# Attention and an ELU feed-forward layer in one kernel: more FFN1 row blocks as seven block products, sums and masks of two head pairs in one instruction, a new order of steps

## The chip, the cores and the metric

The kernel runs on one core of one Trainium2 chip. A core has five engines with queues of their own: TensorE (matmuls, PE in the profile; its weight loads are the row PEld), VectorE (DVE), ScalarE (ACT), GpSimd (POOL, which here starts most DMAs) and SyncE (SP, which starts the other DMAs). The metric is the device time of one execution in microseconds, lower is better. The kernel before took 335.11 us as the median of three runs.

## The reference

For 8 batches and 8 heads, causal attention over 576 positions with 16 beacon keys in front that every query sees, then a feed-forward layer over all 4608 tokens:

```python
B, H, S, Nb, D = (8, 8, 576, 16, 64)
...
scores = scale * np.matmul(q, k_all.transpose(0, 1, 3, 2))
...
scores = np.where(causal, -1000000000.0, scores)
...
a = np.exp(scores)
a /= a.sum(-1, keepdims=True) + 1e-09
return np.matmul(a, v_all).astype(np.float32)
...
x = np.ascontiguousarray(attn_out.transpose(0, 2, 1, 3)).reshape(B * S, H * D)
h = x @ w_in
g = np.where(h > 0.0, h, alpha * (np.exp(np.minimum(h, 0.0)) - 1.0))
return (g @ w_out).astype(np.float32)
```

w_in is 512 x 2048 and w_out 2048 x 512. The 16 + 576 = 592 keys make five blocks of 128 (the last of 80).

## The kernel before, in words

**One long list of steps.** The body defines small functions, each a step, and one string lists all steps in order; `run` calls them one after the other. Each engine takes its instructions from its own queue in that order and waits on semaphores only for data and for buffers. So the string sets which work stands ahead of which on every engine, DMA queues included. `F.4.10` is step F with the arguments 4 and 10.

**Attention.** Heads go in four pairs p, and two head pairs make a half g of a batch. `S` (L308) makes scores, keys on the partitions, in pieces of 2 x 512 columns; `x` (L335) is the exp on ScalarE into the tile `et`; `m` (L340, L346) multiplies the blocks on the diagonal by a triangle of ones on VectorE. A row of et has 1664 columns for one head pair, since keys of later blocks need only later queries: 576, 464, 336, 208 and 80 queries. `L` (L401) sums the exps over the keys: matmuls with a matrix of ones, four heads at a time in strips of 32 output rows (`quad`, L377), then some first products with V. For batches 3 to 7 (`b >= BD`) `D` (L386, L393) first adds the five key blocks on VectorE, so that one matmul per head (L419) does for queries from 112 on. For batches 0 to 2 the quads run over all blocks. `n` (L434, L437) makes 1/sum on ScalarE by Ln and Exp, `W` (L377) multiplies by V, and `M` (L471) scales and writes the tokens, transposed, into the tile xT.

q and k of batches 0 to 2 come by `lq` into staging tiles (qst, kst; two sets) and are transposed by TensorE (`T`). Those of batches 3 to 7 are copied as bf16 to DRAM (`lk`, POOL) and come back through DMA transposes (`lt`, SP, L777) into the second staging set; `lp` (L785, L786) adds the beacon keys there on POOL. `lv` (L141, L144, L149) loads V.

**Feed-forward.** Tokens go in tiles t of 512 (the first is split in two of 256, so t runs from 0 to 9). FFN1 in its plain form is `F` (L502, L511): one block of 128 of the 2048 hidden values, four matmuls of 512 columns into one PSUM bank `hps` (there are two). `e` (L521) and `u` (L526) read it on ScalarE as exp and relu, and `k` (L536) joins them on VectorE to ELU. Four consecutive blocks of hidden values make a row block g. For tiles 8 and 9 the row blocks 0 to 2 are done in another way: the product of the 2 x 2 blocks of weights and of tokens is made of seven block products instead of eight. `H` (L674) makes sums of the weight blocks once, `X` (L687, L690) sums of the token blocks for each tile, `P` (L698, L707) is one product, four matmuls of 256 columns, and a row block has seven (numbers 0 to 6). They alternate between the two banks of `hps`: 0, 2, 4 and 6 into one and 1, 3 and 5 into the other. Between products `K` takes a snapshot of the bank: a copy on ScalarE (L717) after 0, 2 and 3, an add of bank and snapshot on VectorE (L720) after 1, 4 and 5. `E`, `U` (L729, L736) and `V` (L746) are then exp, relu and ELU.

FFN2 is `G` (L557) for tiles 0 and 1. For tiles 2 to 9 it is made of seven block products as well: `Z` and `wt` (L578) make sums on VectorE, `Q` (L632) are the matmuls of 256 columns, and `J` (L646, L650, L653) takes the results out, and the output goes by SP (L656).

Of the kernel before, what the change touches and what calls it, by code (L numbers as in the profile page):

```python
# [9 lines left out]
FP16 = mybir.dt.float16  # L10
BF16 = mybir.dt.bfloat16
# [6 lines left out]
def kernel(  # L18
# [134 lines left out]

# [3 lines left out]
    def load_wi(c):  # L157
        f_ = slice(DF // 2 * c, DF // 2 * (c + 1))
        for g in range(2):
            for i in range(4):  # L160
                nc.gpsimd.dma_start(
                    out=w_in16[32 * i:32 * (i + 1), 2 * g:2 * g + 2, f_], in_=wi_v[i, :, g, :, f_])
# [18 lines left out]
    qks = [konst.tile([P, 2, P * NKC], BF16, name=f"qk{i}") for i in range(2)]  # L181
# [67 lines left out]
    @step  # L249
    def wi(c):  # L250
        load_wi(c)
# [133 lines left out]
    @step  # L385
    def D_(b, p, n, eng="v"):  # L386

        r_ = presum[b, p] = qks[p % 2].bitcast(FP16)[:, :, 0:S]
        t = et(b, p)
        a, e, col = next((a, e, col) for (j, a, e, col) in lays[b] if j == n + 1)  # L390
        rows = kc[n + 1]
        o = r_[0:rows, :, a:e]
        (nc.vector if eng == "v" else nc.gpsimd).tensor_tensor(  # L393
            out=o, in0=t[0:rows, :, a:e] if n == 0 else o, in1=t[0:rows, :, col:col + e - a], op=ALU.add)
# [6 lines left out]
    def L(b, g):  # L401
# [12 lines left out]
        else:  # L414
            t = hd[b, g] = psum.tile([P, 1024], FP32, tag="S", name="lt")
            r_ = lt[b, g] = t[:, 512 - QA:512 - QA + S]
            if b >= BD:
                for i in range(4):
                    nc.tensor.matmul(  # L419
                        out=r_[32 * i:32 * (i + 1), QA:S], lhsT=ones,  # L420
                        rhs=presum[b, 2 * g + i // 2][:, i % 2, QA:S], start=True, stop=True, skip_group_check=True)
# [246 lines left out]

    def rot(n_, t, g, i):
# [4 lines left out]
    def H_(n, g):  # L674
        c = slice(2 * g, 2 * g + 2)
        a11, a12, a21, a22 = (w5[:, j, :, c, i, :] for i in range(2) for j in range(2))
        o_, x_, y_, f_ = {1: (S1[:, :, c], a21, a22, ALU.add), 2: (S2[:, :, c], S1[:, :, c], a11, ALU.subtract),
                          4: (S4[:, :, c], a12, S2[:, :, c], ALU.subtract), 3: (a21, a11, a21, ALU.subtract)}[n]
# [19 lines left out]
    def P_(t, g, ph):  # L698
# [107 lines left out]
    L.0.A T.1.0.0 lv.0.0.1 n.0.A cq.1.0.0 m.0.0.3 T.1.1.0 W.0.A.0 W.0.A.1 M.0.A.0 M.0.A.1 m.0.1.3  # L806
    S.0.2.1 cb.1.2 ck.1.1.0 m.0.2.2 cb.1.0 S.1.5 m.0.2.3 x.0.2.1 wi.0 x.1.5 S.1.3 x.1.3 S.0.3.1
    x.0.3.1 S.0.3.2 x.0.3.2 F.0.1 e.0.1 S.1.1 r.0.1 g.0.1 S.1.4 x.1.4 F.0.0 S.1.2 F.0.2 x.1.1 x.1.2
    u.0.0 lv.0.3.4 lq.1.0.4.8 e.0.2 m.0.3.2 m.0.1.2 m.0.3.3 L.0.B n.0.B e.0.0 wi.1 W.0.B.0 M.0.B.0
    W.0.B.1 M.0.B.1 wo.0 r.0.2 T.1.2.0 F.1.1 ck.1.2.0 g.0.2 T.1.3.0 e.1.1 u.1.1 S.1.6 x.1.6 F.0.4  # L810
    F.1.7 e.0.4 k.0.0 cq.1.3.0 S.1.11 S.1.7 m.1.1.0 cb.1.3 r.0.4 g.0.4 e.1.7 r.1.7 lq.2.0.0.8
    G.0.0.0 x.1.7 F.0.5 x.1.11 e.0.5 S.1.12 g.1.7 cb.2.1 m.1.2.0 x.1.12 S.1.0 F.0.7 r.0.5 G.0.1.0
    S.1.8 x.1.0 g.0.5 F.1.5 e.0.7 x.1.8 m.1.3.1 S.1.10 cb.2.0 m.1.1.1 S.1.9 e.1.5 x.1.10 r.0.7 g.0.7
    cb.2.2 lv.1.0.1 wo.1 r.1.5 g.1.5 x.1.9 F.1.0 u.1.0 e.1.0 m.1.0.0 T.2.0.0 cq.2.0.0 F.0.3 T.2.1.0
    cq.2.1.0 T.2.2.0 e.0.3 u.0.3 m.1.2.1 k.0.3 wt.1.0 k.1.1 ck.2.2.0 F.1.4 F.0.6 e.0.6 S.2.0 S.2.5
    x.2.5 x.2.0 r.0.6 m.1.3.0 G.0.0.1 m.1.0.1 g.0.6 G.0.1.1 k.1.0 lv.1.2.3.4 lp.3.0 lp.3.1 T.2.3.0
    e.1.4 ck.2.3.0 L.1.1 n.1.1 F.1.2 r.1.4 u.1.2 e.1.2 M.1.1.0 W.1.1 M.1.1.1 S.2.3 F.1.3 x.2.3 L.1.0
    W.1.0 n.1.0 wo.2 M.1.0.0 M.1.0.1 u.1.3 e.1.3 wo.3 g.1.4 G.0.0.2 S.2.1 x.2.1 F.2.13 wt.1.1 e.2.13
    S.2.4 lk.3.0 lk.3.1 lt.3.0 x.2.4 S.2.8 x.2.8 k.1.2 cb.2.3 G.0.1.2 F.2.0 u.2.0 u.2.13 S.2.7 x.2.7
    k.1.3 S.2.9 x.2.9 e.2.0 G.0.0.3 o.0.0 G.0.1.3 F.2.3 e.2.3 S.2.10 m.2.0.0 S.2.2 r.2.3 g.2.3 k.2.0  # L820
    x.2.10 x.2.2 G.1.0.0 F.2.11 e.2.11 u.2.11 S.2.6 S.2.12 lv.2.2.3.4 x.2.6 F.2.1 u.2.1 e.2.1
    m.2.1.0 F.1.6 G.1.0.1 m.2.2.1 x.2.12 k.2.13 F.2.7 e.2.7 m.2.0.1 m.2.1.1 k.2.11 u.2.7 k.2.7 u.1.6
    lv.2.0.1 e.1.6 G.1.0.2 S.3.0 x.3.0 S.2.11 x.2.11 F.2.9 F.2.15 e.2.9 H.1.1 o.0.1 u.2.15 k.2.1
    k.1.6 m.2.3.0 e.2.15 L.2.0 W.2.0 n.2.0 F.2.12 m.2.3.1 r.2.9 g.2.9 M.2.0.1 lk.5.1 F.2.6 M.2.0.0
    G.1.0.3 lk.4.0 wt.2.0 wt.2.1 m.2.2.0 e.2.6 u.2.6 wt.4.1 s.0.0 s.0.1 u.2.12 e.2.12 k.2.15 S.3.2
    S.3.3 x.3.3 F.2.4 F.2.14 x.3.2 k.2.12 u.2.14 L.2.1 n.2.1 W.2.1 e.2.4 M.2.1.0 M.2.1.1 e.2.14
    u.2.4 G.1.1.0 S.3.4 F.2.2 lv.3.0.1 F.2.8 k.2.4 k.2.14 x.3.4 k.2.6 e.2.2 u.2.2 e.2.8 r.2.8
    m.3.0.1 S.3.1 o.1.0 k.2.2 lt.3.1 S.3.5 x.3.5 F.2.10 e.2.10 G.1.1.1 x.3.1 u.2.10 G.1.1.2 m.3.0.0
# [115 lines left out]
```

## Time and profile before

| | |
|---|---|
| runs, us | 336.85, 334.85, 335.11 (median 335.11) |
| the profiled execution | 337.32 us, its span 335.6 us |
| TensorE busy | 324.1 us, 97% of the span, 3559 matmuls |
| VectorE busy | 279.1 us, 83% |
| ScalarE busy | 282.4 us, 84% |
| GpSimd busy | 88.7 us, 26% |
| granted TensorE clock | 0.99 |

The profile is of one execution, and its span is what the engines show of it; the time includes a start and an end around it. A busy time counts overlapped instructions once. Matmuls are pipelined, so what one costs in a stream is the distance between starts in the timeline and not its own length. Idle time of an engine that nobody waits for costs nothing. A group's row has line, engine and operation, what it writes and reads with the shapes, the count, then busy us and the mean ns of one, then the idle time in front of it and who ended that.

### The profile page before, as it was taken

To read this page: it belongs to the slowest core of one execution; us is meant where nothing else is said; L and a number is where in the kernel's file an instruction comes from. 1 tells how busy PE (TensorE), PEld (TensorE's weight loads), DVE (VectorE), ACT (ScalarE), POOL (GpSimd) and SP (SyncE) were. 2 spreads that over 40 slices of the span, in tenths; PEclk is the share of its full clock that TensorE was granted. 3 is DMA by queue.
4 is the path that set the end of the run, shared out by engine and by line. 5 is a ranking of instruction groups with operands and counts; after the bars stand their busy time and mean duration, and the time that the engine had idled before them with its cause. 6 is when DMAs were issued, how large, how long until landed. Compare 5 with 4: busy or idle time off the path is not lost. (4 is left out here: it accounts for less than half of the span.)

```text
span 335.6 us, 8729 instructions
## 1 busy us (share of the span) xinstructions
PE 324.1 (97%) x3559; PEld 207.3 (62%) x3561; DVE 279.1 (83%) x592; ACT 282.4 (84%) x463; POOL 88.7 (26%) x121
## 2 busy tenths in 40 slices
PE   7978999999999999999999999999999999999995
PEld 3544766545445555656555666556656788788784
DVE  2662788658799899987999898997999999997971
ACT  2996798899999999989898989897997769879651
POOL 8857768360038404700080060000000000000000
PEclk9996999999999999999999999999999999999999
DMA  8999999999919995997199488000211021020123
GB/s 108 153 170 175 179 186 187 157 145 174 145 32 130 167 170 55 168 172 104 52 111 164 104 58 161 25 31 2 95 33 34 0 97 33 7 89 31 34 87 102
DMA packets 129080, 34.65 MB, mean 103 GB/s; under 512 B 112912, under 2 KB 127504, under 8 KB 129040
## 3 DMA queue, kind: packets, MB, share of 16 engines
q0 software_dynamic: 94912, 18.49, 68.3%
q1 hardware_dynamic: 33552, 15.47, 22.2%
q8 instruction: 28, 0.46, 0.6%
q10 hardware_dynamic: 576, 0.13, 0.2%
q14 instruction: 12, 0.10, 0.1%
HBM read 37.22 MB, written 15.34 MB: 157 GB/s over the span
## 5 line engine op out<-in xcount | busy, mean ns | idle before, releaser
L511 PE MATMUL hps<-xT,w_in 128*128 128x512 f16 (+1 forms) x544 | 120.1, 359 | 1.8 <-DMA w_in<-in_moe_w_in_dram 1.5
L335 ACT ACTIVATE et<-sc 128x1024 f16<-128x1024 f32 (+2 forms) x114 | 104.8, 977 | 5.8 <-PE sc L320 5.8
L632 PEld LDWEIGHTS <-gt 128*128 128x128 f16 x768 | 74.2, 98 | 18.6 <-issue 2.0
L521 ACT ACTIVATE e<-hps 128x512 f32<-128x512 f32 x120 | 72.4, 623 | 9.5 <-PE hps L511 7.9
L511 PEld LDWEIGHTS <-w_in 128*128 128x128 f16 x544 | 50.2, 99 | 46.4 <-issue 8.5
L536 DVE SCALAR_TENSOR_TENSOR gt<-e,r 128x512 f16<-128x512 f32 x108 | 71.7, 684 | 5.5 <-ACT r L526 3.5
L526 ACT ACTIVATE r<-hps 128x512 f16<-128x512 f32 x108 | 64.9, 624 | 7.3 <-PE hps L511 3.8
L632 PE MATMUL ops<-w_out,gt 128*128 128x256 f16 x368 | 47.9, 273 | 0.4 <-DVE osb L650 0.4
L632 PE MATMUL ops<-wt,gt 128*128 128x256 f16 x352 | 46.7, 273 | 0.1
L149 POOL DMA_DIRECT2D v<-in_v_dram x40 | 35.8, 1025 | 5.8 <-DMA w_out<-in_moe_w_out_dram 2.7
L340 DVE TENSOR_TENSOR et<-et,triu 128x512 f16<-128x512 f16 (+4 forms) x108 | 31.8, 332 | 1.7 <-ACT et L335 1.7
L578 DVE TENSOR_TENSOR gt<-gt 128x1024 f16<-128x1024 f16 x48 | 32.5, 685 | 0.5
L377 PEld LDWEIGHTS <-v 128*32 128x32 f16 (+1 forms) x800 | 17.0, 96 | 8.9 <-issue 1.1
L393 DVE TENSOR_TENSOR qk<-qk,et 128x672 f16<-128x672 f16 (+2 forms) x60 | 21.6, 368 | 0.8
L377 PE MATMUL ut<-et,v 128*32 128x464 f16 (+3 forms) x560 | 21.0, 296 | 0.0
L471 DVE TENSOR_TENSOR xT<-ut,rl 128x672 f16<-128x672 f32 (+12 forms) x26 | 16.4, 670 | 1.7 <-ACT rl L437 1.1
L653 DVE TENSOR_TENSOR osb<-ops,sm 128x512 f32<-128x512 f32 x23 | 15.7, 684 | 1.5 <-PE ops L632 1.3
L144 POOL DMA_DIRECT2D v<-in_beacon_v_dram x8 | 6.4, 795 | 37.7 <-PE ut L377 37.7
L557 PE MATMUL ops<-w_out,gt 128*128 128x512 f16 x64 | 16.0, 380 | 0.0
L746 DVE SCALAR_TENSOR_TENSOR gt<-e,r 128x512 f16<-128x512 f32 x24 | 16.0, 686 | 0.0
L632 PE MATMUL ops<-w_out,s 128*128 128x256 f16 x112 | 15.2, 273 | 0.0
L717 ACT COPY kst<-hps 128x512 f32<-128x512 f32 x18 | 10.3, 588 | 5.5 <-PE hps L707 5.3
(112 smaller groups left out, 406.1 us busy)
## 6 DMA issues: line engine op xcount, KB each, us to landing
out_dram<-osb SPq DMA_DIRECT2D x35, 256.0 KB, 2.3
v<-in_v_dram POOLq DMA_DIRECT2D x24, 128.0 KB, 8.2
scr<-in_q_dram POOLq DMA_DIRECT2D x5, 576.0 KB, 14.5
scr<-in_k_dram POOLq DMA_DIRECT2D x5, 576.0 KB, 16.1
w_in<-in_moe_w_in_dram POOLq DMA_DIRECT2D x16, 128.0 KB, 6.7
w_out<-in_moe_w_out_dram POOLq DMA_DIRECT2D x4, 512.0 KB, 9.5
v<-in_v_dram POOLq DMA_DIRECT2D x8, 112.0 KB, 9.7
v<-in_v_dram POOLq DMA_DIRECT2D x8, 80.0 KB, 8.2
```

The costliest lines, as they stand in the source:

```text
L149: nc.gpsimd.dma_start(out=vt[b][r0:r0 + n, j, :, :], in_=v[b, :, ilo[j]:ilo[j] + n, :].rearrange("h s d -> s h d"),)
L335: nc.scalar.activation(out=ets[b, d][:, :, a - EC2 * d:e - EC2 * d], in_=sc[b, g][:, :, a - c0:e - c0], func=AFT.Exp, bias=0.0, scale=SCALE)
L340: nc.vector.tensor_tensor(out=o, in0=o, in1=i, op=ALU.mult)
L377: nc.tensor.matmul(out=t[32 * i:32 * (i + 1), a - qa:e - qa], lhsT=ones[0:kc[j], :] if half is None else v16[0:kc[j], j, h, 32 * half:32 * ...
L393: (nc.vector if eng == "v" else nc.gpsimd).tensor_tensor(out=o, in0=t[0:rows, :, a:e] if n == 0 else o, in1=t[0:rows, :, col:col + e - a], ...
L471: nc.vector.tensor_tensor(out=x_tile(k)[:, 2 * g:2 * g + 2, tok - TT * k:to - TT * k], in0=u[:, :, o - qa:o - qa + w], in1=rls[b, g][:, o: ...
L511: nc.tensor.matmul(out=h[:, n_, :], lhsT=w_in16[:, cc, P * fc:P * (fc + 1)], rhs=xt[k][:, cc, a - TT * k:e - TT * k], start=(cc == 0), sto ...
L521: nc.scalar.activation(out=eb[t, i], in_=flat(hp[t, i]), func=AFT.Exp, bias=0.0, scale=1.0)
L526: nc.scalar.activation(out=rb[t, i], in_=flat(hp[t, i]), func=AFT.Relu, bias=0.0, scale=1.0)
L536: nc.vector.scalar_tensor_tensor(out=half(t, i), in0=eb[t, i], scalar=1.0, in1=rb[t, i], op0=ALU.subtract, op1=ALU.min)
L578: (nc.vector if eng == "v" else nc.gpsimd).tensor_tensor(out=o_, in0=a_, in1=b_, op=op_)
L632: nc.tensor.matmul(out=xy[t, n_][qd], lhsT=lw[:, P * qd:P * (qd + 1)], rhs=wt_[:, c, :], start=(first and c == 0 and (qd == 0 or (t, n_) n ...
```

## The change

1. Row block 0 of tiles 4 to 7 and row block 3 of tiles 8 and 9 go from F, e, u, k to P, K, E, U, V. X runs for tiles 4 to 7 too, and H for row block 3, whose weight sums lie in the q staging tile of the second set (`more`).
2. `D` takes two head pairs in one instruction, and runs for batches 1 and 2 too; L uses the result wherever there is one. The sums of batches 1 and 2 lie in the staging tiles, the others in `qk01`, which joins two tiles.
3. `m` takes two head pairs in one instruction, for batches from 1 on.
4. The beacon row of V is loaded behind the first block of V instead of ahead of all; `load_wi` and `load_v` are split, so that each DMA is a step of its own.
5. The string of steps has a new order. Up to `cq.1.3.0` it is the old one but for the split loads; from there on it is new.

```diff
     def load_v(b, js):
...
-            nc.gpsimd.dma_start(
-                out=vt[b][0:NB, 0, :, :], in_=beacon_v[b].rearrange("h n d -> n h d"))
         for j in js:
...
+            if j == 0:
+                nc.gpsimd.dma_start(
+                    out=vt[b][0:NB, 0, :, :], in_=beacon_v[b].rearrange("h n d -> n h d"))
...
-    qks = [konst.tile([P, 2, P * NKC], BF16, name=f"qk{i}") for i in range(2)]
+    qk01 = konst.tile([P, 2, 2, P * NKC], BF16, name="qk01")
+    qks = [qk01[:, i, :, :] for i in range(2)]
...
     def m(b, p, g):
 
-        t = et(b, p)
+        t = et(b, p) if b == 0 else None
         if b > 0:
-            m_ = lambda c: triu[:, c:c + 2, :].unsqueeze(1).broadcast_to([P, 2, 2, P])
+            t = ets[b, p].rearrange("p h (y c) -> p h y c", y=2)
+            m_ = lambda c: triu[:, c:c + 2, :].unsqueeze(1).unsqueeze(1).broadcast_to([P, 2, 2, 2, P])
...
-    def D_(b, p, n, eng="v"):
-
-        r_ = presum[b, p] = qks[p % 2].bitcast(FP16)[:, :, 0:S]
-        t = et(b, p)
+    def D_(b, g, n):
+
+        if b < BD:
+            r_ = stq[b % 2][g].bitcast(FP16)[:, 0:4 * S].rearrange("p (y i s) -> p y i s", y=2, i=2)
+        else:
+            r_ = qk01.bitcast(FP16)[:, :, :, 0:S]
+        presum[b, g] = r_
+        t = ets[b, g].rearrange("p i (y c) -> p y i c", y=2)
         a, e, col = next((a, e, col) for (j, a, e, col) in lays[b] if j == n + 1)
         rows = kc[n + 1]
-        o = r_[0:rows, :, a:e]
-        (nc.vector if eng == "v" else nc.gpsimd).tensor_tensor(
-            out=o, in0=t[0:rows, :, a:e] if n == 0 else o, in1=t[0:rows, :, col:col + e - a], op=ALU.add)
+        o = r_[0:rows, :, :, a:e]
+        nc.vector.tensor_tensor(
+            out=o, in0=t[0:rows, :, :, a:e] if n == 0 else o, in1=t[0:rows, :, :, col:col + e - a], op=ALU.add)
...
-            if b >= BD:
+            if (b, g) in presum:
                 for i in range(4):
                     nc.tensor.matmul(
                         out=r_[32 * i:32 * (i + 1), QA:S], lhsT=ones,
-                        rhs=presum[b, 2 * g + i // 2][:, i % 2, QA:S], start=True, stop=True, skip_group_check=True)
+                        rhs=presum[b, g][:, i // 2, i % 2, QA:S], start=True, stop=True, skip_group_check=True)
...
+    more = {id(y): stq[1][0].bitcast(FP16)[:, 512 * i:512 * (i + 1)].rearrange("p (k c f) -> p k c f", k=2, f=P)
+            for i, y in enumerate((S1, S2, S4))}
+
+    def wsum(y, g):
+        return y[:, :, 2 * g:2 * g + 2] if g < SG else more[id(y)]
...
-                lw = w5[:, a_[1], k_, 2 * g + c, a_[0], :] if isinstance(a_, tuple) else a_[:, k_, 2 * g + c, :]
+                lw = w5[:, a_[1], k_, 2 * g + c, a_[0], :] if isinstance(a_, tuple) else wsum(a_, g)[:, k_, c, :]
```

In the string, by numbers of steps: F and e from 120 to 96, u and k from 108 to 84, P from 42 to 84, K from 36 to 72, E, U and V from 24 to 48 each, X from 8 to 24, H from 12 to 16, D from 80 to 56 (now for two head pairs each), m from 68 to 40. All others keep their number. Some places of the new order:

```diff
+    F.1.3 T.2.1.0 wo.3 cq.2.0.0 T.2.3.0 e.1.3 u.1.3 F.1.2 lk.3.0 e.0.3 cq.2.1.0 ck.2.3.0 L.1.0 S.2.5
...
+    X.4.4 S.4.9 S.4.7 D.4.0.0 Z.3.3.0 Q.2.84.91 D.4.0.1 P.4.0.0 Q.2.91.98 Z.3.3.1 H.3.0 e.3.9 x.4.9
...
+    x.6.11 u.6.9 Q.4.77.84 e.6.9 P.6.0.0 S.6.7 S.6.9 J.4.4 lv.6.4 D.6.0.1 Q.4.84.91 K.6.0.0 x.6.9
+    x.6.7 D.6.0.2 k.5.15 Q.4.91.98 P.6.0.1 D.6.0.3 J.4.5 lp.7.1 P.6.0.2 K.6.0.2 Q.4.98.105 S.7.5
...
+    Q.5.14.21 x.7.4 K.6.0.4 K.6.0.5 J.5.0.v k.6.12 P.6.0.6 Z.5.2.0 E.6.0.6 F.6.4 lv.6.0 L.6.0
```

More of the change, by code (lines that the diff above doesn't have):

```diff
@@ L152, in load_v, with load_wi @@
             )
+            if j == 0:
+                nc.gpsimd.dma_start(
+                    out=vt[b][0:NB, 0, :, :], in_=beacon_v[b].rearrange("h n d -> n h d"))
     wi_v = moe_w_in.rearrange("(g i t d) f -> i d g t f", i=4, t=2, d=32)
     wo_v = moe_w_out.rearrange("(f p) m -> p f m", p=P)
-    def load_wi(c):
+    def load_wi(c, n):
         f_ = slice(DF // 2 * c, DF // 2 * (c + 1))
[L159 to L162, printed above, removed]
+        g, i = n // 4, n % 4
+        nc.gpsimd.dma_start(
+            out=w_in16[32 * i:32 * (i + 1), 2 * g:2 * g + 2, f_], in_=wi_v[i, :, g, :, f_])
     def load_wo(i):
@@ L249, in wi @@
     @step
-    def wi(c):
-        load_wi(c)
+    def wi(c, n):
+        load_wi(c, n)
     @step
@@ L676, in H_ @@
         a11, a12, a21, a22 = (w5[:, j, :, c, i, :] for i in range(2) for j in range(2))
-        o_, x_, y_, f_ = {1: (S1[:, :, c], a21, a22, ALU.add), 2: (S2[:, :, c], S1[:, :, c], a11, ALU.subtract),
-                          4: (S4[:, :, c], a12, S2[:, :, c], ALU.subtract), 3: (a21, a11, a21, ALU.subtract)}[n]
+        s1, s2, s4 = (wsum(y, g) for y in (S1, S2, S4))
+        o_, x_, y_, f_ = {1: (s1, a21, a22, ALU.add), 2: (s2, s1, a11, ALU.subtract),
+                          4: (s4, a12, s2, ALU.subtract), 3: (a21, a11, a21, ALU.subtract)}[n]
         for kk_ in range(2):
@@ L811 @@
[L811 to L816, printed above, removed]
@@ L911 @@
[L911 to L914 removed]
+    L.0.A T.1.0.0 lv.0.0 lv.0.1 n.0.A cq.1.0.0 m.0.0.3 T.1.1.0 W.0.A.0 W.0.A.1 M.0.A.0 M.0.A.1
+    m.0.1.3 S.0.2.1 cb.1.2 ck.1.1.0 m.0.2.2 cb.1.0 S.1.5 m.0.2.3 x.0.2.1 wi.0.0 wi.0.1 wi.0.2 wi.0.3
@@ new lines @@
+    E.9.0.6 V.9.0.1 Q.8.0.7 P.9.1.0 Z.8.3.1 P.9.1.1 E.9.0.5 K.9.1.0 V.9.0.4 Q.8.7.14 K.9.1.1
+    U.9.0.5.v V.9.0.6 P.9.1.2 Z.8.1.1 J.7.6 P.9.1.3 Q.8.14.21 K.9.1.2 K.9.1.3 P.9.1.4 Z.8.1.0
+    E.9.1.1 P.9.1.5 Q.8.21.28 K.9.1.4 U.9.1.1 Z.8.2.0 K.9.1.5 J.8.0 P.9.1.6 Q.8.28.35 E.9.1.6
+    U.9.1.6 P.9.2.0 Z.8.2.1 Q.8.35.42 K.9.2.0 V.9.1.1 U.9.1.4 J.8.1 P.9.2.1 E.9.1.4 V.9.1.6 E.9.1.5
+    K.9.2.1 V.9.1.4 P.9.2.2 Q.8.42.49 J.8.2 Z.8.4.0 K.9.2.2 V.9.0.5 Q.8.49.56 U.9.1.5 P.9.2.3
+    Q.8.56.63 K.9.2.3 P.9.2.4 E.9.2.1 Z.8.4.1 P.9.2.5 Q.8.63.70 U.9.2.1 K.9.2.4 K.9.2.5 V.9.2.1
@@ L915 @@
+    Q.9.80.88 J.9.4 Q.9.88.96 Q.9.96.104 J.9.5 Jh.9.0 Q.9.104.112 Jh.9.1
     """)
```

212 lines of the change are left out of this document (106 added, 106 removed).

## The prediction

> **What bounds the kernel now.** I read the page's first part, then the busy times by stretch of the span, then the timeline of TensorE, then the groups by form, then the waits. Busy time on the page:
>
> ```profile
> PE 324.1 (97%) x3559; PEld 207.3 (62%) x3561; DVE 279.1 (83%) x592; ACT 282.4 (84%) x463; POOL 88.7 (26%) x121
> ```
>
> A share over the whole span hides stages, so the same by stretches (length, then busy us and count of PE, PEld, DVE, ACT, POOL, then clock, DMA share, GB/s):
>
> ```profile
> 0.00:45.00 45.00, 38.30 (x612) 22.77 (x615) 23.16 (x68) 32.73 (x45) 32.30 (x57) 0.92 1.23 159
> 45.00:100.00 55.00, 54.67 (x695) 28.95 (x695) 41.80 (x87) 51.33 (x80) 21.46 (x20) 1.00 1.70 143
> 100.00:240.00 140.00, 139.07 (x1427) 83.86 (x1428) 130.50 (x284) 128.38 (x210) 34.92 (x45) 1.00 1.02 106
> 240.00:300.00 60.00, 60.00 (x558) 44.90 (x556) 59.29 (x118) 49.41 (x92) 0.00 (x0) 1.00 0.12 40
> 300.00:336.00 36.00, 32.06 (x277) 26.79 (x274) 24.32 (x40) 20.51 (x41) 0.00 (x0) 1.00 0.20 67
> ```
>
> After 45 us TensorE is idle for 0.33 + 0.93 us up to 240 and not at all up to 300, at full clock: it sets the pace. The second thing to see is VectorE: 59.29 of 60 us from 240 to 300 without TensorE losing anything, but already 93% from 100 to 240. Whatever the change takes from TensorE it must not hand to VectorE beyond that.
>
> A busy matmul row is pipelined, so prices of matmuls come from spacing in the timeline (start, length, engine, what, count):
>
> ```profile
> 150.75 1.90 PE L511 MATMUL hps<-xT,w_in 128*128 128x512 f16 x8
> 162.28 1.50 PE L377 MATMUL ut<-et,v 128*32 128x464 f16 x40
> 163.71 0.94 PE L632 MATMUL ops<-w_out,gt 128*128 128x256 f16 x7
> 300.88 0.60 PE L707 MATMUL hps<-qst,hi 128*128 128x256 f16 x4
> 301.32 0.60 PE L707 MATMUL hps<-qst,lo 128*128 128x256 f16 x4
> 301.75 0.93 PE L632 MATMUL ops<-w_out,gt 128*128 128x256 f16 x7
> ```
>
> Four matmuls of 256 columns start every 0.44 and 0.43 us: 109 ns each. Eight of 512 last 1.90 us; less the last one's own 0.38 (the first form row below), seven spacings take 1.52, 217 ns each. The 40 matmuls of L377 are ten quads, four at a time in strips of 32 output rows, 2 x 1552 = 3104 columns in 163.71 - 162.28 = 1.43 us: 0.461 ns a column.
>
> **The change, part by part.** Durations, from the groups by form (count, then busy us, mean ns), and one row of the waits:
>
> ```profile
> L511 PE MATMUL hps<-xT,w_in 128*128 128x512 f16 x416 | 102.1, 380 | 0.3 <-DVE gt L548 0.3
> L340 DVE TENSOR_TENSOR et<-et,triu 128x512 f16<-128x512 f16 x56 | 23.1, 417 | 1.7 <-ACT et L335 1.7
> L340 DVE TENSOR_TENSOR et<-et,triu 80x160 f16<-80x160 f16 x32 | 7.4, 231 | 0.0
> L393 DVE TENSOR_TENSOR qk<-et 128x928 f16<-128x928 f16 x20 | 12.6, 633 | 0.1
> L393 DVE TENSOR_TENSOR qk<-qk,et 128x672 f16<-128x672 f16 x20 | 10.0, 502 | 0.2
> L393 DVE TENSOR_TENSOR qk<-qk,et 128x416 f16<-128x416 f16 x20 | 7.3, 370 | 0.2
> L393 DVE TENSOR_TENSOR qk<-qk,et 80x160 f16<-80x160 f16 x20 | 4.4, 234 | 0.3
> L720 DVE TENSOR_TENSOR kst<-hps,kst 128x512 f32<-128x512 f32 x9 | 6.2, 688 | 1.8 <-ACT kst L717 1.8
> L690 DVE TENSOR_TENSOR qst<-xT 128x512 f16<-128x512 f16 x4 | 1.7, 421 | 0.0
> L578 DVE TENSOR_TENSOR hi<-lo,w_in 128x256 f16<-128x256 f16 x6 | 1.5, 285 | 0.0
> PEld L419 <- DVE qk L393: 1.5, 3, 0.6
> ```
>
> *FFN1 blocks on TensorE.* Six more row blocks (one each in tiles 4 to 7, one more each in 8 and 9) go from four F steps, 16 matmuls of 512 (16 x 217 = 3.47 us), to seven P steps, 28 of 256 (28 x 109 = 3.05). 0.42 each, on the path: -2.5 us.
>
> A rule of the Trainium skill speaks against this: "TensorE: Matmul & The Clock Gate", section "Back-to-back issue gap", gives a sustained stream of load and matmul pairs 131 ns at 512 columns and 81 at 128. By that, an estimate of 98 for 256 by a straight line, a block would go from 2.10 to 2.74 us, and the six would cost 3.8 us instead. The trace has 217 and 109, so I do not follow it.
>
> *Sums on TensorE.* For batches 1 and 2, four L steps stream one presummed row of 464 columns instead of 1552: 1088 x 0.461 ns = 0.50 us each, -2.0 us.
>
> *VectorE.* Wider forms by the slope of the rows, (633 - 370)/(928 - 416) = 0.514 ns a column. Sums D: a pair of head pairs takes 1110 + 847 + 584 + 316 = 2857 ns where two singles took 2 x 1739. Batches 3 to 7: 10 x 2.86 - 20 x 1.74 = -6.2; batches 1 and 2, new: 4 x 2.86 = +11.4. Masks: per head pair 2 x 417 + 231 = 1065, joined 2 x 680 + 313 = 1673: 28 x 1.065 - 14 x 1.673 = -6.4 (-1.8 in batches 1 and 2). X for tiles 4 to 7: 16 x 0.421 = +6.7. K adds: 18 x 0.688 = +12.4. H, two each for four new block sums: 8 x 0.285 = +2.3. The closing operation of an ELU costs the same in k and V (684 and 686). In all +20.2, or 299 us busy.
>
> By stretch: 45 to 100 gets 11.4 - 1.8: 51.4 us of work in 55 - 2.0 = 53.0. From 100 to 240: -6.2 - 4.6 + 6.7 + 8.3 + 2.3 = +6.5, 137.0 in 140 - 4 x 0.42 = 138.3, 99.1%. From 240 to 300 half of the last six adds: 61.4 in 59.6. At the 98.8% that VectorE reaches (59.29 of 60) the last two need 138.7 and 62.1: 0.4 and 2.5 us more than TensorE. The 2.5 can slide into 300 to 336, where VectorE is idle for 11.7; cover gone, it costs all 2.9, and 0 if everything slides. I take 0.8, nearer nothing because of those 11.7.
>
> *ScalarE.* 18 K copies of 588 ns (the row of L717): +10.6, 7.1 of it from 100 to 240: 135.5 in 138.3. Hidden behind TensorE, barely: what is lost if not belongs to the third rival. E and U swap e and u one for one at 623 to 641 ns: nothing.
>
> *Waits added.* L of batches 1 and 2 now waits for the D chain. Ten sums of batches 3 to 7 cost 1.5 us, three waits, the longest 0.6; four more at the same mean are 0.6, between 0 and 4 x 0.6 = 2.4. Queued behind a waiting L are the W and F steps of TensorE, and ScalarE waits for these.
>
> *Moved DMAs and queues.* Up to cq.1.3.0 (about 40 us) the order is the same but for the beacon V row of each batch, now behind the first V piece: one POOL issue of 0.5 us later, within 0.5 us either way, taken as 0. The split of wi keeps its order. SP: the first transpose of batch 3 now also waits for L of batch 1, since its sums lie in that staging; both precede S.3.0 by some 11 us of matmuls, and a transpose lands in 3.8 to 8.6: 0. POOL: behind lp.7.1, which waits for S.6.9, stands the first V piece of batch 6. From S.6.9 to L.6.0 TensorE has 10.4 us of matmuls and such a piece lands in 9.7 (median of the issues): 0, but up to 6 late at the longest landing of 16.6. If late, L.6.0 is.
>
> **Sum.** -2.5 - 2.0 + 0.8 + 0.6 = -3.1. The profiled execution took 337.3 us with a span of 335.6, so 334.2 for it; its runs have a median of 335.1, 2.2 lower, so 332.0. A measurement of this kernel tells about 1% from no change: faster is below 331.8, slower above 338.5.
>
> **The rivals.**
> *VectorE takes over.* 99% over 140 us leaves no room; a wait on it costs at once. For: ScalarE and VectorE both at 98% or more there. Against: 240 to 300. Whole overhang 2.9 and sum waits 2.4: 335.1 - 4.5 + 5.3 = 335.9; 334 to 338.
> *The adds hold TensorE.* An F bank of these tiles is freed by ScalarE alone. In a P block two banks alternate: of products 0 to 6, numbers 3 and 6 and the next user of the bank come after a K add on VectorE, numbers 2, 4 and 5 after a K copy on ScalarE. An add that stands behind one more operation of 0.69 in VectorE's queue keeps the next product waiting. For: twelve of the 18 come where VectorE is 99% busy. Against: for the 18 adds of before only ScalarE waited, 2.8 us; TensorE lost nothing, as other matmuls lie between. 18 x 0.69 = 12.4: 344.4. It is slower by over 1% once an add costs 6.5/18 = 0.36 us. 339 to 345.
> *The new order closes gaps.* 1.3 us idle after 45 us and, an estimate, as much under pipelined ends; with no overhang: 335.1 - 4.5 + 0.6 - 2.6 = 328.6; 328.5 to 331.
> *No saving in the products.* A load takes 98 ns under a matmul of 109. If the 72 extra ones stand open, 7.1 us: 335.1 - 2.0 + 1.4 - 2.5 + 7.1 = 339.1. The page named above points that way; the 0.44 and 0.43 us speak against it.
>
> **How the numbers follow.** Forecast 0.50, 330.8 to 333.5, some 0.22 of it below 331.8; VectorE 0.17; adds 0.12; gaps closed 0.18; no saving 0.03. So faster 0.40, within 1% 0.45, slower 0.15. The range 328.8 to 339.0 leaves out the far half of the adds and a little below.
>
> **What would show it.** P steps spaced 109 ns; the L steps of batches 1 and 2 with four matmuls of 464; VectorE near 299 us busy and 98% or more from 100 to 240; TensorE idle under 2 us between 45 and 300; waits of PEld on the sums near 2 us. Wrong: TensorE waiting on K adds for several us, an L step on V, or VectorE idle while TensorE waits.

## The result, and the profile after

The changed kernel is slower by half a percent: 338.13 us as the median of 22 runs (335.90 to 341.88) beside 335.62 for 22 runs of the kernel before, ratio 1.0057 [1.0038, 1.0077]. Twelve more runs gave 1.0026 [1.0001, 1.005]. The forecast was 332.0, a gain of 0.9%. The medians are of all runs, while the ratios leave out the few of each kernel that fell into a slower state of the chip.

The profiled execution of it took 335.9 us with a span of 334.2, which is less than the 337.3 and 335.6 shown of before. That is the start: from 0 to 45 us the granted clock was 0.92 in the profile of before and 1.00 in this one. So I compare from a mark behind the start, the normalisation `n.0.B` at the end of batch 0, which both kernels reach by the same matmuls. Its rows in the timeline of ScalarE (start, length), before:

```profile
34.09 0.70 ACT L434 ACTIVATE rl<-lt 128x640 f32<-128x640 f32 x1 [0.19 <-PE lt L377]
```

and after:

```profile
30.16 0.70 ACT L442 ACTIVATE rl<-lt 128x640 f32<-128x640 f32 x1
```

From there to the end of the span: 335.6 - 34.1 = 301.5 us before, 334.2 - 30.2 = 304.0 after. This has the sign and about the size of the medians.

The page's first part and the stretches of the changed kernel (columns as in the prediction):

```profile
PE 320.7 (96%) x3567; PEld 213.2 (64%) x3569; DVE 299.8 (90%) x568; ACT 291.3 (87%) x481; POOL 93.0 (28%) x121
...
0.00:45.00 45.00, 39.13 (x633) 23.38 (x636) 27.70 (x74) 35.67 (x48) 31.19 (x53) 1.00 1.27 164
45.00:100.00 55.00, 51.88 (x617) 27.06 (x616) 49.04 (x90) 48.31 (x76) 28.27 (x29) 1.00 2.11 167
100.00:240.00 140.00, 139.60 (x1469) 89.18 (x1467) 137.80 (x253) 135.84 (x224) 33.56 (x39) 1.00 0.85 94
240.00:300.00 60.00, 59.85 (x582) 47.16 (x581) 59.87 (x113) 50.36 (x94) 0.00 (x0) 1.00 0.13 43
300.00:336.00 36.00, 30.27 (x275) 26.43 (x272) 25.42 (x42) 21.11 (x42) 0.00 (x0) 0.97 0.19 63
```

VectorE came out at the 299 us forecast, with 137.8 of 140 and 59.87 of 60 us in the stretches that looked dangerous, and TensorE loses 0.40 and 0.15 us there. What is new is in the second row: TensorE is idle for 3.12 us between 45 and 100, where it had been idle for 0.33. The costs of the parts were near the forecast; groups by form, and three rows of the timeline:

```profile
L341 DVE TENSOR_TENSOR et<-et,triu 128x1024 f16<-128x1024 f16 x28 | 18.8, 681 | 0.0
L735 DVE TENSOR_TENSOR kst<-hps,kst 128x512 f32<-128x512 f32 x18 | 12.3, 683 | 0.5 <-PE hps L722 0.4
L401 DVE TENSOR_TENSOR qst<-et 128x1856 f16<-128x1856 f16 x2 | 2.2, 1117 | 0.0
L401 DVE TENSOR_TENSOR qst<-qst,et 128x1344 f16<-128x1344 f16 x2 | 1.7, 854 | 0.0
```

```profile
171.23 0.60 PE L722 MATMUL hps<-qst,hi 128*128 128x256 f16 x4
171.67 0.93 PE L640 MATMUL ops<-wt,gt 128*128 128x256 f16 x7
...
55.08 0.38 PE L427 MATMUL lt<-qst,ones 128*32 128x464 f16 x4
```

A product of four matmuls still takes 0.44 us, and L of batch 1 is four matmuls of 464 columns. One row of the waits has grown from a single wait of 0.3 us in the kernel before (`gt L548` there), while the sums themselves hold up the loads of L only twice (waiter, releaser: us in total, times, longest):

```profile
PE hps L519 <- DVE gt L556: 4.0, 5, 2.3
...
PEld L427 <- DVE qk L401: 0.6, 1, 0.6
PEld L427 <- DVE kst L401: 0.4, 1, 0.4
```

L556 is the step g, in the second way to close an F step: after the exp on ScalarE, `r` (L551) and `g` both run on VectorE, and only g, the maximum of bank and r, lets the bank of `hps` go. Tiles 0 and 1 use it for nine blocks. The timeline of VectorE there:

```profile
42.51 1.11 DVE L401 TENSOR_TENSOR qst<-et 128x1856 f16<-128x1856 f16 x1
43.54 0.42 DVE L551 TENSOR_SCALAR r<-e 128x512 f16<-128x512 f32 x1
44.06 0.69 DVE L556 TENSOR_TENSOR gt<-hps,r 128x512 f16<-128x512 f32 x1
44.67 1.48 DVE L401 TENSOR_TENSOR qst<-qst,et 128x1344 f16<-128x1344 f16 x2
46.06 0.42 DVE L551 TENSOR_SCALAR r<-e 128x512 f16<-128x512 f32 x1
46.59 0.69 DVE L556 TENSOR_TENSOR gt<-hps,r 128x512 f16<-128x512 f32 x1
47.20 2.37 DVE L551 TENSOR_SCALAR r<-e 128x512 f16<-128x512 f32 x1
49.49 0.47 DVE L586 TENSOR_TENSOR lo<-w_in 128x256 f16<-128x256 f16 x2
49.89 0.15 DVE L276 TENSOR_TENSOR qk<-bkT 128x16 bf16<-128x16 bf16 x1
49.96 0.15 DVE L276 TENSOR_TENSOR hi<-bkT 128x16 bf16<-128x16 bf16 x1
50.04 0.31 DVE L401 TENSOR_TENSOR qst<-qst,et 80x320 f16<-80x320 f16 x1
50.28 0.91 DVE L341 TENSOR_TENSOR et<-et,triu 128x1024 f16<-128x1024 f16 x2
51.11 0.68 DVE L556 TENSOR_TENSOR gt<-hps,r 128x512 f16<-128x512 f32 x1
```

of TensorE:

```profile
44.81 1.03 PE L519 MATMUL hps<-xT,w_in 128*128 128x256 f16 x8 [0.44 <-DVE gt L556]
...
51.84 1.03 PE L519 MATMUL hps<-xT,w_in 128*128 128x256 f16 x8 [2.33 <-DVE gt L556]
```

and of GpSimd:

```profile
46.80 2.24 POOL L785 DMA_DIRECT2D scr<-in_q_dram  x1
```

Two things are to be seen. The sums of batch 1 (qst, L401) stand between the r and g operations without a gap. And one r of 0.42 us took 2.37: it began 0.40 us after GpSimd began to issue a copy, and lasted 0.53 us longer than that issue. Between this r and its g the new order has put 1.6 us of other work: weight sums, beacon keys, the last sum of this half of batch 1 (0.31 us) and masks (0.91 us). The g came out at 51.8, and TensorE had waited 2.33 us for its bank.

### The profile page after: what moved, and what is told of

It is laid out like the page before. It is cut to its first block, busy times and chain, and to the rows that moved or that the text cites. A ratio compares the mean times of both kernels' runs of the same rounds, so it can differ in the third digit from the quotient of the medians.

```text
span 334.2 us, 8753 instructions
## 1 busy us (share of the span) xinstructions
PE 320.7 (96%) x3567; PEld 213.2 (64%) x3569; DVE 299.8 (90%) x568; ACT 291.3 (87%) x481; POOL 93.0 (28%) x121
## 5 line engine op out<-in xcount | busy, mean ns | idle before, releaser
L336 ACT ACTIVATE et<-sc 128x1024 f16<-128x1024 f32 (+2 forms) x114 | 106.3, 1003 | 3.3 <-PE sc L321 3.3
L519 PE MATMUL hps<-xT,w_in 128*128 128x512 f16 (+1 forms) x448 | 94.9, 349 | 4.5 <-DVE gt L556 4.0
L529 ACT ACTIVATE e<-hps 128x512 f32<-128x512 f32 x96 | 60.9, 648 | 6.5 <-PE hps L519 5.6
L519 PEld LDWEIGHTS <-w_in 128*128 128x128 f16 x448 | 41.3, 97 | 39.2 <-issue 8.9
L534 ACT ACTIVATE r<-hps 128x512 f16<-128x512 f32 x84 | 52.6, 645 | 2.1 <-PE hps L519 1.1
L147 POOL DMA_DIRECT2D v<-in_v_dram x40 | 38.4, 1000 | 51.6 <-PE lt L381 30.3
L640 PE MATMUL ops<-w_out,gt 128*128 128x256 f16 x368 | 49.0, 273 | 0.0
L341 DVE TENSOR_TENSOR et<-et,triu 128x1024 f16<-128x1024 f16 (+5 forms) x66 | 26.8, 446 | 0.0
L732 ACT COPY kst<-hps 128x512 f32<-128x512 f32 x36 | 21.3, 594 | 5.7 <-PE hps L722 5.2
L722 PEld LDWEIGHTS <-w_in 128*128 128x128 f16 x192 | 18.8, 98 | 2.4 <-issue 0.2
L401 DVE TENSOR_TENSOR qk<-qk,et 128x1344 f16<-128x1344 f16 (+2 forms) x30 | 17.5, 583 | 0.2
```

The costliest lines, as they stand in the source:

```text
L147: nc.gpsimd.dma_start(out=vt[b][r0:r0 + n, j, :, :], in_=v[b, :, ilo[j]:ilo[j] + n, :].rearrange("h s d -> s h d"),)
L336: nc.scalar.activation(out=ets[b, d][:, :, a - EC2 * d:e - EC2 * d], in_=sc[b, g][:, :, a - c0:e - c0], func=AFT.Exp, bias=0.0, scale=SCALE)
L341: nc.vector.tensor_tensor(out=o, in0=o, in1=i, op=ALU.mult)
L519: nc.tensor.matmul(out=h[:, n_, :], lhsT=w_in16[:, cc, P * fc:P * (fc + 1)], rhs=xt[k][:, cc, a - TT * k:e - TT * k], start=(cc == 0), sto ...
L529: nc.scalar.activation(out=eb[t, i], in_=flat(hp[t, i]), func=AFT.Exp, bias=0.0, scale=1.0)
L534: nc.scalar.activation(out=rb[t, i], in_=flat(hp[t, i]), func=AFT.Relu, bias=0.0, scale=1.0)
```

## The experiments

The kernel before had medians of 335.4 to 336.0 beside these runs. The theories, by the letters that the expectations use. A: r operations stretched while GpSimd issues a copy. B: VectorE full from 85 us on. C: the sums of batch 1 overfill VectorE at 38 to 65 us, and g, which frees the banks, stands behind them. The table has, for each kernel, its runs, its ratio to the kernel before, and from its trace TensorE's idle time from 38 to 100 us and the time from the mark to the end.

| kernel | median us (runs) | ratio | idle 38 to 100 | mark to end |
|---|---|---|---|---|
| before | 335.62 (22) | 1 | 0.33 | 301.5 |
| after | 338.13 (22) | 1.0057 [1.0038, 1.0077] | 4.40 | 304.0 |
| again | 336.78 (12) | 1.0026 [1.0001, 1.005] | 4.24 | 304.4 |
| no_masks | 338.26 (9) | 1.0037 [0.9999, 1.0074] | 3.80 | 305.3 |
| no_d1 | 334.37 (12) | 0.9958 [0.993, 0.9986] | 1.29 | 301.5 |
| no_d1_again | 336.08 (12) | 0.9998 [0.997, 1.0027] | 0.85 | 301.1 |
| no_d12 | 334.95 (12) | 0.9987 [0.9963, 1.0011] | 1.01 | 301.5 |
| r1port_before | 336.27 (12) | 1.002 [0.9995, 1.0045] | 0.71 | 302.2 |
| r1port_after | 336.95 (12) | 1.0048 [1.0026, 1.007] | 4.45 | 303.8 |
| r1port_no_d1 | 335.14 (12) | 0.9974 [0.9955, 0.9993] | 1.83 | 301.9 |
| uk | 337.22 (6) | 1.0068 [1.0044, 1.0092] | 2.77 | 302.0 |
| uk_again | 336.72 (12) | 1.0021 [0.9997, 1.0046] | 3.86 | 303.0 |
| uk_no_d1 | 335.81 (12) | 1.0018 [1.0, 1.0036] | 2.47 | 302.3 |
| uk_r1port | 335.86 (12) | 1.0002 [0.9971, 1.0032] | 2.74 | 302.0 |
| r1port_undo_p | 362.12 (5) | 1.0781 [1.0753, 1.081] | | |

**The changed kernel once more** (again), unchanged.

> The changed kernel unchanged, for a second profile beside the kernel before on the same chip. Theory A (one collision): the loss sits in one place, 45 to 50 us, where a TENSOR_SCALAR r of VectorE lasted 2.37 us instead of 0.43 while POOL issued the copy of q to DRAM (46.80 to 49.04 us); a second profile shows such a long r again, of 1 us or more in excess, and TensorE idle 2 us or more near it. Theory B (VectorE too full): the loss is spread; VectorE is again 98 to 100% busy from 100 to 300 us and TensorE's distance from its matmul prices is 2 us or more greater than in before over that stretch. Time 337 to 339 us by both.

1.0026, and 304.4 us from the mark. Its trace lost as much, in another place: VectorE, GpSimd, TensorE,

```profile
77.40 3.36 DVE L551 TENSOR_SCALAR r<-e 128x512 f16<-128x512 f32 x1 [0.99 <-ACT e L529]
80.79 0.69 DVE L556 TENSOR_TENSOR gt<-hps,r 128x512 f16<-128x512 f32 x1
```

```profile
76.09 4.41 POOL L785 DMA_DIRECT2D scr<-in_k_dram  x2 [4.40 <-issue]
```

```profile
81.53 1.03 PE L519 MATMUL hps<-xT,w_in 128*128 128x256 f16 x8 [1.84 <-DVE gt L556]
```

Here r lasted 3.36 us under two issues in a row, and ended 0.26 us after them. From 38 to 65 us TensorE was idle for 1.60 us instead of 4.14, and from 65 to 100 for 2.64 instead of 0.27. So the slowdown repeats, and the stretched r decides where a part of it falls.

**Without the sums of batch 1** (no_d1). L.1.0 and L.1.1 run over all blocks again.

```diff
-    k.1.1 ... F.0.5 D.1.0.0 r.0.7 ... lv.1.3 D.1.0.1 e.0.5 F.1.4 S.1.7 D.1.0.2 r.0.5 ... D.1.0.3 ck.2.2.0 ...
-    ... e.1.2 D.1.1.0 k.0.3 D.1.1.1 F.1.0 ... W.1.0 D.1.1.2 D.1.1.3 L.1.1 ...
+    (the same without D.1.*)
```

> Without the sums D of batch 1, so that L of batch 1 streams five blocks again, as in before: TensorE does 2 x 0.50 = 1.0 us more, VectorE 5.7 us less, all of it between 40 and 65 us. Theory A: r and g come earlier in VectorE's queue there but r still meets POOL; 0 to 2 us faster than the changed kernel, since the stretch from 40 to 65 us loses its overload. Theory B: the rest of the span stays as full as it is, so the 1.0 us of matmuls counts: 0 to 1 us slower.

Faster than the changed kernel, 0.9958 against 1.0057 and 1.0026, and 2.5 to 2.9 us less from the mark. The stretch from 38 to 100 us, first after, then this kernel:

```profile
38.00:100.00 62.00, 57.60 (x673) 30.47 (x668) 55.62 (x102) 54.98 (x85) 29.91 (x32) 1.00 2.05 170
```

```profile
38.00:100.00 62.00, 60.71 (x722) 32.65 (x723) 50.90 (x99) 56.98 (x89) 32.49 (x35) 1.00 1.99 169
```

TensorE works 3.1 us more in the same time, 0.9 of it the longer L steps. Of the five waits on g two are left, 0.7 us in all; one of them, at 39 us, lies ahead of the sums and is no effect of them (0.84 us in the changed kernel, 0.53 here). That settles which part of the change costs, and not yet how.

**Without the masks of batches 3 to 7** (no_masks): 16.7 us less for VectorE, all of it after 85 us.

```diff
-    m.3.0.0 ... m.3.0.1 ... m.7.1.0 m.7.1.1 ...
```

> Leaves out the causal masks of batches 3 to 7: 10 x 1.67 = 16.7 us less on VectorE between about 85 and 245 us, nothing less on the other engines. Theory B: VectorE's queue is what holds TensorE there; TensorE gets back the 2 us or more that it loses beyond its matmul prices, 2 to 4 us faster. Theory A: at most 0.7 us faster, as VectorE's fullness alone costs nearly nothing after 50 us.

```profile
100.00:240.00 140.00, 138.60 (x1458) 87.73 (x1456) 126.25 (x225) 135.07 (x223) 30.80 (x41) 1.00 0.85 94
240.00:300.00 60.00, 59.92 (x587) 46.91 (x585) 58.77 (x110) 50.70 (x94) 0.00 (x0) 1.00 0.13 42
```

VectorE now has 14 us free from 100 to 240, and nothing is gained: 1.0037, and five waits on g of 3.6 us in all, as in the changed kernel. (Of the 305.3 us from the mark a part is the clock, which was 0.97 from 45 to 100 us in this profile. From 100 us on it was 1.00, and TensorE was idle for 1.40 us up to 240, not less than the 0.40 of the changed kernel.) Theory B falls.

**r in another form.** `r` gets a second operand (a row of ones), which takes 0.684 us instead of 0.42.

```diff
-        nc.vector.tensor_scalar(
-            out=rb[t, i], in0=eb[t, i], scalar1=1.0, scalar2=1.0, op0=ALU.min, op1=ALU.subtract)
+        nc.vector.scalar_tensor_tensor(
+            out=rb[t, i].rearrange("p (a b) -> p a b", b=32), in0=eb[t, i].rearrange("p (a b) -> p a b", b=32),
+            scalar=1.0, in1=ones.unsqueeze(1).broadcast_to([P, 16, 32]), op0=ALU.min, op1=ALU.subtract)
```

In the changed kernel (r1port_after), in the kernel before (r1port_before) and in the one without the sums of batch 1 (r1port_no_d1):

> The changed kernel with r, min(e, 1) - 1, as SCALAR_TENSOR_TENSOR against a broadcast tile of ones instead of TENSOR_SCALAR: 12 x (0.68 - 0.43) = 3.0 us more on VectorE. Theory A (r collides with POOL): no r lasts over 0.75 us while POOL issues a copy of 2.2 us, the runs lie closer together than 334.3 to 339.6 us, and it is 1 to 3 us faster than the changed kernel in spite of the added work. The Trainium skill, 'SBUF — State Buffer', section 'Who interferes with whom', says that tensor_scalar can enter a two-port mode and then shuts out GpSimd or is shut out by it, and that a form with two SBUF inputs meets only GpSimd's reads. Theory C (the sums of batch 1 overfill VectorE from 40 to 65 us, whatever r does): 0 to 2 us slower than the changed kernel.

> The kernel before with the same rewriting of r. Its profile shows one long r (1.73 us at 72 us). Theory A: the collision costs it less than it costs the changed kernel: within 1 us of the kernel before, and the changed kernel with the new r is 0 to 3 us faster than this. Theory C: within 1 us too, but the changed kernel with the new r is slower than this by 2 us or more.

> The changed kernel without the sums D of batch 1 (TensorE 1.0 us more, VectorE 5.7 us less from 40 to 65 us) and with the new r. Without the sums alone it was 0.68% faster than the changed kernel. Theory A: that gain came from r, which runs ahead of POOL's copy when 2.6 us of sums no longer stand in front of it; with the new r the sums of batch 1 no longer cost, so this is 0 to 1.5 us slower than the changed kernel with the new r. Theory C: the gain is that of VectorE's load and stays, 1 to 3 us faster than the changed kernel with the new r.

No r lasts over 0.69 us in these three, though some begin under the same copies; VectorE and GpSimd of r1port_after:

```profile
77.02 0.68 DVE L551 SCALAR_TENSOR_TENSOR r<-e,ones 128x512 f16<-128x512 f32 x1
```

```profile
75.30 4.41 POOL L786 DMA_DIRECT2D scr<-in_k_dram  x2
```

So the stretching can be had or not by the form of r. But the twelve r cost 12 x 0.26 = 3.1 us more on VectorE, and the changed kernel gains little (303.8 from the mark, and not the 1 to 3 us that theory A expected): its waits on g are still five of 3.8 us in all, the longest 1.2, four of them spread over 40 to 53 us. Theory A alone is not the loss. The sums of batch 1 cost 303.8 - 301.9 = 1.9 us here too, with no r stretched, and the runs of the same chip agree (1.0048 with them, 0.9974 without), as theory C had it.

**Back to F for row block 0 of tiles 4 to 7** (r1port_undo_p), to price the block products.

```diff
-    ... P.4.0.0 ... K.4.0.0 ... U.4.0.1 E.4.0.1 ... V.4.0.1 ... X.4.1 ...
+    ... F.4.0 e.4.0 u.4.0 k.4.0 ... F.4.1 e.4.1 u.4.1 k.4.1 ... (where V stood)
```

> The changed kernel with the new r, and row block 0 of tiles 4 to 7 back to four F steps each in the places where V stood (their X and K steps are gone, H of this block comes before tile 8): TensorE 4 x 0.42 = 1.7 us more, VectorE 12 x 0.69 + 16 x 0.42 = 15.0 us less between 100 and 260 us, ScalarE 7.1 us less. If the block products deliver what was summed: 1 to 4 us slower than the changed kernel with the new r (1.7 and what the makeshift places cost). If the K adds and the fuller VectorE hold TensorE as in the rival of the prediction: equal or faster.

```profile
ACT e L529 <- PE hps L519: 24.8, 24, 3.1
...
PE hps L519 <- ACT r L534: 10.6, 10, 1.2
```

362.12 us, which says nothing of the products: each of the 16 F steps stands, with its own e, u and k right behind it, where a V stood, and TensorE waits ten times, 10.6 us in all, until ScalarE lets a bank go. The rest of the 25 us more than r1port_after is not placed. Inconclusive.

**u and k for r and g in five F steps** of tiles 0 and 1 (uk): now u on ScalarE lets the bank go, and all sums stay.

```diff
-    ... r.1.7 g.1.7 ... r.1.5 g.1.5 ... r.0.7 ... g.0.7 ... r.0.5 ... g.0.5 r.1.4 ... g.1.4 ...
+    ... u.1.7 k.1.7 ... u.1.5 k.1.5 ... u.0.7 ... k.0.7 ... u.0.5 ... k.0.5 u.1.4 ... k.1.4 ...
```

> The changed kernel with five F steps' endings moved from VectorE to ScalarE: row blocks 7, 5 and 4 of tile 1 and 7 and 5 of tile 0 are closed by u and k instead of r and g, so that the bank of an F step is freed by u on ScalarE and not by g on VectorE, behind the sums. All sums of batch 1 stay. VectorE loses five operations of about 0.43 us and five of 0.7 us change kind; ScalarE gets five of about 0.6 us, in a stretch (45 to 55 us) where it is idle for nearly 4 us. Theory C (VectorE has more work than matmuls give it time for at 38 to 65 us, and g, which frees the bank, stands behind it): the wait of TensorE on g of L556 goes or falls below 1 us, TensorE's idle time from 38 to 65 us falls from near 4 us towards 1.5, and the time is 1.5 to 3.5 us below the changed kernel's, 333.5 to 336. Theory A alone (the one long r under a POOL issue): the r that collided is gone from 47 us but the r at 76 us is left, so 0.5 to 2 us less. Theory E (the sums of batch 1 cost by the L steps that wait for them, not by what stands behind them on VectorE): within 0.5 us of the changed kernel.

> The kernel with five F steps closed by u and k once more, unchanged. Its first trace and its six runs disagree: from the normalisation that ends batch 0 to the end the trace took 302.0 us against 304.0 and 304.4 in the two traces of the changed kernel, but the time of its runs was no lower; its trace spent 3 us more than theirs before that point, where the program is the same and the granted clock was lower (0.91 in the first 38 us). Theory C (the sums of batch 1 hold up what frees the banks): that stretch takes 301.5 to 302.5 us again, and the runs come to a ratio of 0.999 to 1.003 to the kernel before. If the start was no chance and goes with this edit: a slow start again, and 1.005 to 1.008.

The first trace takes 302.0 us from the mark, 2.0 less than after, and its waits on g are down to one of 0.8. The median of its six runs was no lower, the second set was at 1.0021, and the second trace took 303.0. In both traces one r at 80 us was stretched (1.45 and 1.85), and in the second another at 91 us (1.15); there TensorE idles 1.85 us from 65 to 100. A part of the loss goes with this edit, as theory C has it, but by the runs alone the part is not sure. The runs (337.22 and 336.72 us, beside 338.13 and 336.78 of the changed kernel) do not rule out theory E, the traces speak against it: the loads of L waited longer for the sums than in the trace of after (1.2 us on `kst` against 0.4), and the time from the mark was shorter.

**Both edits** (uk_no_d1: u and k, no sums of batch 1; no_d12: as after, without the sums of batches 1 and 2).

> As the run before it, and without the four sums of batch 1 as well, so that the L steps of that batch stream four rows of 464 columns again (2.0 us more on TensorE) while VectorE has 5.7 us less. Theory C: with the room on VectorE made in both ways, TensorE waits on no VectorE operation from 38 to 65 us in either, so the sums are now worth their 1 us on TensorE (two pairs of head pairs, 2 x 0.50): this kernel is 0.3 to 1.2 us slower than the one with the sums and u, k endings. If room is still lacking there, this one is the faster, by up to 1 us, and near the changed kernel without the sums, 333 to 335: the candidate to beat both kernels.

> The changed kernel without the sums of batches 1 and 2: all four L steps of these batches stream four rows of 464 columns, as in the kernel before. TensorE +2.0 us of matmuls, VectorE -11.4 us. Theory C: the sums of batch 2 fall at 65 to 95 us, where VectorE has room in the changed kernel (TensorE idle 0.5 us there), so they pay their 1.0 us: this kernel is 0.3 to 1.2 us slower than the one without the sums of batch 1 alone, 334.5 to 336. Rival (sums before 100 us never pay): as fast as that one or faster, 333 to 334.5.

uk_no_d1 gains nothing on no_d1 (302.3 from the mark), although VectorE has room: ScalarE is now busy for 9.75 of the 10 us from 45 to 55, so the bound has only moved. That is how I read it; no run shows it by itself. (The 2.0 us more on TensorE in that expectation should be 1.0, two L steps of 0.50.) My expectation that the sums would pay once g is out of the way failed: from the mark 302.0 and 303.0 with them, 302.3 without, and by the runs of the same chip the kernel with them was the slower (1.0068 against 1.0018), by its second set level (1.0021). no_d12 is level with no_d1 (301.5, and 301.5 and 301.1): the sums of batch 2, put where TensorE was idle for 0.3 us in 35, neither gain nor lose what can be told here, though they take 0.9 us of matmuls from TensorE.

**The version that came out fastest, once more** (no_d1_again).

> The changed kernel without the sums of batch 1, once more, on the same chip as the run before it: the version that came out fastest. If its 0.9958 holds: 0.993 to 0.999, and 301 to 302 us from the normalisation that ends batch 0 to the end, as in its first trace (301.5) and in that of the kernel before (301.5). Rival: its gain was the luck of its starts, and it measures 0.999 to 1.002, since by that stretch alone it is no faster than the kernel before.

0.9998 [0.997, 1.0027] after 0.9958: the rival holds. It is level with the kernel before or faster by a few tenths of a percent, more can't be said. Two sets lie below 1 with their whole interval (no_d1 and r1port_no_d1), the repeat of no_d1 does not, and no trace is shorter from the mark than that of before by more than 0.4 us. So no version here beats the kernel before for sure.

**Both cures** (uk_r1port): u and k in five F steps, and the form with ones for the seven r that are left. All sums stay.

> Both cures at once: five F steps of tiles 0 and 1 closed by u and k on ScalarE's side, and the seven r operations that are left (one at 76 to 91 us met POOL's copy in every trace of the changed kernel with u and k) in the form with a second operand, which was never lengthened. All sums stay. If the sums of batch 1 cost by these two things alone (banks freed late behind them, and r stretched while POOL issues a copy), no r lasts over 0.75 us, TensorE idles 2.5 us or less from 38 to 100 us, and from the normalisation that ends batch 0 to the end it takes 301.0 to 302.0 us, as the changed kernel without these sums did (301.5 and 301.1); its runs come to a ratio of 0.997 to 1.002. If something third is behind the loss, that stretch stays at 302.5 to 304 us and the ratio at 1.002 to 1.006.

```profile
38.00:100.00 62.00, 59.26 (x684) 31.59 (x682) 54.36 (x101) 58.28 (x92) 30.87 (x33) 1.00 2.03 168
```

1.0002 [0.9971, 1.0032], 302.0 us from the mark, the upper edge of what was expected if these two things are all; the idle time of 2.74 us is a little over the 2.5. The two together take back 2.0 of the 2.5 to 2.9 us that leaving the sums out takes back. The last 0.5 us or more I did not place.

## Why the prediction was wrong, point by point

**What failed: "45 to 100 gets 11.4 - 1.8: 51.4 us of work in 55 - 2.0 = 53.0."** The sum was right on average and wrong as a test of fit. The sums of batch 1 do not spread over 55 us. In the trace they run from 42.5 to 60.0 us, and they fall in front of g. From 38 to 65 us VectorE is busy for 25.0 of 27 us against 20.7 before, and TensorE is idle for 4.14 us against 0.07 (first before, then after):

```profile
38.00:65.00 27.00, 26.93 (x432) 17.60 (x431) 20.73 (x44) 24.25 (x37) 16.28 (x18) 1.00 1.81 178
```

```profile
38.00:65.00 27.00, 22.86 (x350) 14.56 (x345) 25.04 (x44) 21.16 (x30) 11.68 (x13) 1.00 1.87 180
```

So the step that failed is the overhang of this stretch: the sum put it at nothing, and it came to 3.12 us of idle time between 45 and 100 us, 4.40 from 38 us on. The r and g operations were visible in the code and in the trace of before, and the working did not ask whose bank waits behind a sum.

**"Waits added": wrong queue.** The forecast priced the waits of L of batches 1 and 2 on the sums, 0.6 us. They came to 0.4 us (the row with kst) in the first trace and 1.2 in the second. What had to be priced was the queue on the other side: the operations behind the sums on VectorE, and TensorE, which waits for these. In the traces, sums of batch 1 cost 304.0 - 301.5 = 2.5 and 304.4 - 301.1 = 3.3 us as the change has them, against -1.0 forecast for that batch; the other -1.0, of batch 2, did not show in the time either (no_d12). The rival "VectorE takes over" had the right engine but the wrong place: it was put at 100 to 300 us.

**r under the copies: missed.** The group of L543 in the page of before had a mean of 533 ns for an operation that takes 0.42, and its timeline has one of 1.73 us at 72 us, with TensorE behind it:

```profile
72.23 1.73 DVE L543 TENSOR_SCALAR r<-e 128x512 f16<-128x512 f32 x1 [1.39 <-ACT e L521]
```

```profile
74.74 1.90 PE L511 MATMUL hps<-xT,w_in 128*128 128x512 f16 x12 [0.26 <-DVE gt L548]
```

I read the 533 ns as a price and not as a warning. There it cost TensorE only 0.26 us, since g came right behind r; it is the `gt L548` of the first row by forms in the prediction.

**What was right.** TensorE's own work: I give each matmul of the traces its spacing (216 ns for 512 columns, 109 for 256, in proportion between, a quarter in strips of 32). From the mark to the end the sum of these prices falls by 4.3 us of the 4.5 forecast. VectorE's total (299.8 for 299), the 137.8 us from 100 to 240 (137.0), ScalarE's 135.8 (135.5), the forms' prices (1117, 854, 681 ns for 1110, 847, 680) all held. The ceiling of 98.8% for VectorE was too low: it reached 99.8% from 240 to 300. "No saving in the products" fell: four matmuls take 0.44 us. The moved DMAs cost nothing: the longest wait of TensorE or its loads on a DMA is 0.4 us after and 1.5 before.

**The overhang: the right size, and not for the reason given.** From the normalisation of batch 3 (`n.3.0`) to the end it is 220.7 us before and 219.7 after, while the price there falls by 1.9. So 0.9 of it was given back, where 0.8 was taken for a VectorE that is too full. But from n.3.0 to its last matmul TensorE is idle for 0.99 us before and 0.97 after, and with 11 us less for VectorE there (no_masks) the stretch took 220.7, no less. That the number fits is in part luck. What the trace of after does show is the rival "The adds hold TensorE", in small:

```profile
280.42 0.68 DVE L735 TENSOR_TENSOR qst<-hps,kst 128x512 f32<-128x512 f32 x1
```

```profile
280.53 0.60 PE L722 MATMUL hps<-xT,hi 128*128 128x256 f16 x4
281.16 0.60 PE L722 MATMUL hps<-qst,w_in 128*128 128x256 f16 x4
```

The second product begins 0.06 us after the add ends and 0.63 us after the first product, where 0.44 is usual. Four products start so, behind an add, 0.06 to 0.30 us late (at 263.5, 270.5, 281.2 and 313.8 us), 0.7 us in all against 0.04 before, and the trace of again has the same four. The views of waits have no row for them: by the modelled ends of its matmuls TensorE is hardly idle there. The rival had put a wait of 0.69 us at each of 18 adds. The last few tenths of the 0.9 are not placed.

**Where the gain went, in one line:** from the mark to n.3.0 80.9 us became 84.3 for 2.4 us less of matmuls. Without the sums of batch 1 it is 81.5. That still is 0.6 more than before for 1.5 us less of matmuls, 2.1 us in all. TensorE's idle time there accounts for 0.9 of it (1.71 us against 0.77); the rest, in the new order of steps between 30 and 115 us, stays open. In sum, from the mark: -4.3 of matmuls, +3.7 by the sums of batch 1 (2.8 of time and the 0.9 of matmuls that they save), +2.1 open, +0.9 behind n.3.0, which makes +2.4 where 2.5 was measured.

## What to carry to other kernels

When work is moved to an engine with room, test the room where the work will stand, in a window as long as the work's own neighbours and not in the stage's average, and ask which buffer is freed by the operation that comes to stand behind it. An engine may be 99.8% busy over 60 us without harm if nothing that it frees is wanted soon (59.87 us here, 0.15 us lost), and cost 2.5 to 3.3 us at 93% over 27 where it frees a matmul's bank. When profiled executions differ in their start, compare from a common step.

## What the runs showed of the hardware

A TENSOR_SCALAR of 0.42 us on VectorE lasted 2.37, 3.36 and, before, 1.73 us when it began while GpSimd was issuing a copy between two places in DRAM (2.2 us an issue), and it ended 0.25 to 0.53 us after the issue. In the nine traces that have such a meeting twelve began 0.4 to 1.8 us behind the start of an issue and lasted 0.71 to 3.36 us. Two began 0.11 and 0.22 us behind the start (uk at 77.37 us, again at 46.35) and took 0.42. The same calculation as SCALAR_TENSOR_TENSOR took 0.68 to 0.69 us beside the same issues, every time. The Trainium skill, page "SBUF — State Buffer", section "Who interferes with whom", has the rule: tensor_scalar can go into a mode that takes the port pair which VectorE and GpSimd share, and who comes second is blocked until the first is done. The long ones agree with it (0.42 to 2.37 and 3.36 us here); the two that began just behind the start of an issue and were not held do not show it, and why is not known from these runs.
